# The last token group's first layer as pairs of 64-row matmuls into two banks

## The chip, the cores and the metric

One NeuronCore of a Trainium2 chip runs the whole program. The metric is the device time of one execution in microseconds. The kernel before has two recorded times, 681.75 and 683.06, with a median of 682.4.

## What is computed

Sparse attention over 4 batches, 8 heads, 768 positions and a head size of 64 feeds a two-layer block with 512 inputs, 2048 hidden units and 512 outputs. Cut to what matters here:

```python
x = attn_out.transpose(0, 2, 1, 3).reshape(3072, 512)   # tokens x model width
h = x @ w_in                                             # 512 -> 2048
sp = np.where(h > 20.0, h, np.log1p(np.exp(np.minimum(h, 20.0))))
g = h * np.tanh(sp)                                      # Mish
out = g @ w_out                                          # 2048 -> 512
```

The attention looks at a window of 16 positions to each side and at one summary (largest key, mean value) of each block of 32. It comes before the part that changes.

## The kernel before, in words

The 3072 tokens are twelve chunks of 256 (`CH`); two chunks make a token group of 512 (`TG`), so there are six groups, 0 to 5 (`NG`). The hidden width is cut into 16 blocks of 128 (`NFC`). A step is one group and one hidden block, 96 steps in all, group after group.

Precision comes from splitting. Each activation and each weight is held as a high and a low part of type float32r (`xh`, `xl`, `ah`, `al`, and weights `hi`, `lo`), and a product of two numbers is three matmuls: high by high, high weight by low activation, low weight by high activation.

For step (g, fc):

- `ff_in` (line 346) takes one PSUM tile `ph` of 128 x 512 from the pool `ps_w` and accumulates 12 matmuls into it on line 352: four pieces of 128 rows of the model width (`NCC`) by three products. The stationary operand is 128 x 128 of `w_in`, the moving operand 128 rows by 512 tokens of x. All 128 rows of the array are contracted at once.
- `ff_act` (line 356) applies Mish on ScalarE straight from `ph` into the tile `a` in SBUF, on line 359.
- `ff_split` (line 362) makes `ah` (a cast, line 368) and `al` (a subtraction on VectorE, line 370). From group 1 on both stand on VectorE.
- `ff_out` (line 372) does 12 matmuls on line 380, for four blocks of 128 tokens by three products. They accumulate over all 16 steps of the group into the four PSUM tiles `po` of the pool `ps_o`. After the last step of the group the results are copied out on line 388 and written by DMA on line 389.

The order of the work is written out by hand (`tc.manual_schedule()`): each engine works in the order of the code. The last loop (line 451) calls, for its index i, `ff_in` and `ff_act` of step i, then attention work for a later group where there is some, `ff_split` of step i, and `ff_out` of step i - 2. So on TensorE two steps' matmuls lie between a step's `ff_in` and its own `ff_out`: `ff_out(i-2)`, `ff_in(i+1)`, `ff_out(i-1)` and `ff_in(i+2)`, until the last steps, where `ff_in` has run out.

Attention for group g is worked off during group g - 1, so steps 80 to 95 (group 5) hold none of it. In the earlier groups three attention pieces stand between the long matmuls on TensorE: the scores (line 283: 64-row, 64-column pieces, where the two heads use the upper and the lower half of the array and write two PSUM tiles), the transposes (line 320) and the values (line 338: 120 rows, 64 columns). float32 matmuls of these lines run as two instructions each.

Each of the two PSUM pools has four tiles of one bank. The pool `ps_w` serves `ph` and the scores, transposes and values of the attention.

Of the kernel before, what the change touches and what calls it, by code (L numbers as in the profile page):

```python
# [9 lines left out]
F32 = mybir.dt.float32  # L10
# [3 lines left out]
AF = mybir.ActivationFunctionType  # L14
# [3 lines left out]
B, H, S, D = 4, 8, 768, 64  # L18
DM, DFF = 512, 2048
BLK, WIN = 32, 16  # L20
P = 128
# [9 lines left out]
NCC = DM // P  # L31
# [6 lines left out]
TG = CG * CH  # L38
NG = NCH // CG
# [17 lines left out]
def fused_kernel(ctx: ExitStack, tc: tile.TileContext, q0, qk, kt, v0, vw, vs, w_in, w_out, out):  # L57
    nc = tc.nc
# [10 lines left out]
    ps_w = ctx.enter_context(tc.tile_pool(name="ps_w", bufs=4, space=PS))  # L69
# [9 lines left out]
    for h in range(2):  # L79
        r = slice(h * QT, (h + 1) * QT)  # L80
# [23 lines left out]
    def weight(w, part, fc):  # L104

        group, k = (early, fc) if fc < EARLY else (late, fc - EARLY)
        return group[w][part][:, k, :]
# [60 lines left out]
    for part, step, at0 in ((blocks[:, :NQ], QT, -WIN), (blocks[:, NQ:], P, CH)):  # L168
        n = part.shape[1]
# [6 lines left out]
    part = blocks[:, :NQ]  # L176
# [166 lines left out]
    st = {}  # L343
    po = {}

    def ff_in(g, fc):
        xh, xl = xs[g]
        ph = ps_w.tile([P, TG], F32, tag="w", name=f"ph{g}_{fc}")
        wh, wl = (weight(0, part, fc) for part in range(2))
        for cc in range(NCC):  # L350
            for n, (w, x) in enumerate(((wh, xh), (wh, xl), (wl, xh))):
                nc.tensor.matmul(ph, w[:, cc * P:(cc + 1) * P], x[:, cc, :],  # L352
                                 start=(cc == 0 and n == 0), stop=(cc == NCC - 1 and n == 2))
        st[g, fc] = ph

    def ff_act(g, fc):

        a = ff.tile([P, TG], F32, tag="t", name=f"a{g}_{fc}", bufs=2)
        nc.scalar.activation(a, st[g, fc], AF.Mish)  # L359
        st[g, fc] = a  # L360

    def ff_split(g, fc):
# [33 lines left out]
    for u, unit in enumerate(todo[CG * HP:]):  # L396
        g, u = divmod(u, CG * HP)
# [15 lines left out]
    n = CG * HP  # L413
# [37 lines left out]
    for i in range(len(steps) + 2):  # L451
        upper_weight()
        if i < len(steps):
            ff_in(*steps[i])
            ff_act(*steps[i])
            if i < NFC:
                waiting.append(ff_split(*steps[i]))
# [72 lines left out]
```

## Time and profile before

| what | value |
|---|---|
| times recorded | 681.75 and 683.06 us, median 682.4 |
| span of the profiled execution | 680.6 us |
| TensorE matmul (PE) busy | 644.6 us, 95% |
| ScalarE (ACT) busy | 333.4 us, 49% |
| VectorE (DVE) busy | 291.1 us, 43% |
| mean granted TensorE clock over the span | 0.971 |
| stretch 585 to 668 us (most of group 5): granted clock | 1.00 |
| the same stretch: ACT busy, DVE busy | 10.18 us and 18.11 us of 83.00 |

The page names no time for the profiled execution other than its span, from the first to the last instruction; the recorded times lie 1.2 and 2.5 us above it.

A row of the timeline gives the start and the length of an instruction, or of a run of like ones with their count (x16), then engine, line, operation and tiles. PE is the matmul, PEld the load of its weights, which can run while an earlier matmul streams. A matmul's length reaches from its start until its last result is written; the next one may begin before that, so the distance from start to start tells what one costs in a row of them. In `128*128 128x512` the first pair is rows by columns of the weights, the second the moving operand. A bracket at the end gives the idle time before and what ended it.

### The profile page before, as it was taken

To read this page: it belongs to the slowest core of one execution; us is meant where nothing else is said; L and a number is where in the kernel's file an instruction comes from. 1 tells how busy PE (TensorE), PEld (TensorE's weight loads), DVE (VectorE), ACT (ScalarE), POOL (GpSimd) and SP (SyncE) were. 2 spreads that over 40 slices of the span, in tenths; PEclk is the share of its full clock that TensorE was granted. 3 is DMA by queue.
4 is the path that set the end of the run, shared out by engine and by line. 5 is a ranking of instruction groups with operands and counts; after the bars stand their busy time and mean duration, and the time that the engine had idled before them with its cause. 6 is when DMAs were issued, how large, how long until landed. Compare 5 with 4: busy or idle time off the path is not lost.

```text
span 680.6 us, 10882 instructions
## 1 busy us (share of the span) xinstructions
PE 644.6 (95%) x4160; PEld 514.8 (76%) x4160; DVE 291.1 (43%) x836; ACT 333.4 (49%) x722; POOL 67.5 (10%) x119
## 2 busy tenths in 40 slices
PE   4767888999999999999999999999999999999997
PEld 3546676777788788788788788788788788888886
DVE  3987889982332334442322344442232232221112
ACT  2766776685555545555545555545455445111111
POOL 3230001111010010010010010010010010000000
PEclk9967979899999999999999999999999999999999
DMA  8895556742141124351121144331141110010001
GB/s 290 235 301 180 192 177 233 240 122 87 51 146 46 50 71 153 116 175 46 50 85 45 48 134 152 117 114 45 45 152 45 45 60 1 15 47 0 1 1 62
DMA packets 31252, 71.05 MB, mean 104 GB/s; under 512 B 4832, under 2 KB 9952, under 8 KB 31200
## 3 DMA queue, kind: packets, MB, share of 16 engines
q1 hardware_dynamic: 31200, 70.35, 32.4%
q8 instruction: 33, 0.54, 0.4%
q14 instruction: 19, 0.16, 0.1%
HBM read 61.54 MB, written 6.29 MB: 100 GB/s over the span
## 4 chain that ended last, share of the span: by engine, by line
PE 82%; ACT 8%; DVE 4%; DMA 3%; issue 1%; SPq 0%; POOL 0%; POOLq 0%; ACTq 0%; DVEq 0%
PE po L380 37%; PE ph L352 35%; PE x_ps L338 4%; PE sc L283 3%; PE pt_ps L320 3%; ACT w_f L143 2%; DVE w_f L156 2%; DVE w_f L154 1%; DMA qk<-qk 1%; ACT pr L303 1%; DMA vw<-vm 1%; DMA vw<-vw 1%; ACT L359 1%; ACT L303 1%; ACT a L359 1%
## 5 line engine op out<-in xcount | busy, mean ns | idle before, releaser
L359 ACT ACTIVATE a<-ph 128x512 f32<-128x512 f32 x96 | 57.4, 598 | 155.9 <-PE ph L352 155.5
L368 DVE CAST ah<-a 128x512 fp32r<-128x512 f32 x80 | 34.0, 426 | 197.1 <-ACT a L359 197.1
L380 PE MATMUL po<-w_early_out_hi,ah 128*128 128x512 f32 x240 | 98.6, 411 | 0.0
L352 PE MATMUL ph<-xh,w_early_in_hi 128*128 128x512 f32 x240 | 97.8, 407 | 0.0
L359 ACT ACT_TABLE_LOAD x41 | 52.6, 1283 | 88.6 <-PE ph L352 88.4
L380 PE MATMUL po<-w_early_out_lo,ah 128*128 128x512 f32 x240 | 95.3, 397 | 0.0
L352 PE MATMUL ph<-xl,w_early_in_hi 128*128 128x512 f32 x240 | 95.0, 396 | 0.0
L352 PE MATMUL ph<-xh,w_early_in_lo 128*128 128x512 f32 x240 | 94.9, 395 | 0.0
L380 PE MATMUL po<-w_early_out_hi,al 128*128 128x512 f32 x240 | 94.7, 394 | 0.0
L314 POOL TENSOR_TENSOR pr<-pr,rs 128x480 f32<-128x480 f32 x48 | 48.2, 1005 | 421.7 <-DVE rs L313 361.1
L303 ACT ACTIVATE pr<-pr,nm 128x120 f32<-128x120 f32 x192 | 73.6, 384 | 9.7 <-DVE nm L298 9.1
L340 DVE TENSOR_TENSOR xl<-x_ps,xh 128x256 fp32r<-128x256 f32 x48 | 20.3, 423 | 118.1 <-ACT xh L339 118.0
L370 DVE TENSOR_TENSOR al<-a,ah 128x512 fp32r<-128x512 f32 x96 | 66.3, 691 | 2.7
L380 PE MATMUL po<-w_late_out_hi,ah 128*128 128x512 f32 x144 | 58.5, 407 | 0.0
L352 PE MATMUL ph<-xh,w_late_in_hi 128*128 128x512 f32 x144 | 57.6, 400 | 0.0
L380 PE MATMUL po<-w_late_out_lo,ah 128*128 128x512 f32 x144 | 57.0, 396 | 0.0
L380 PE MATMUL po<-w_late_out_hi,al 128*128 128x512 f32 x144 | 56.8, 394 | 0.0
L352 PE MATMUL ph<-xh,w_late_in_lo 128*128 128x512 f32 x144 | 56.2, 391 | 0.0
L352 PE MATMUL ph<-xl,w_late_in_hi 128*128 128x512 f32 x144 | 56.1, 390 | 0.0
L380 PEld LDWEIGHTS po<-w_early_out_hi,ah 128*128 128x128 f32 x240 | 45.9, 191 | 13.0 <-issue 4.1
L352 PEld LDWEIGHTS ph<-xh,w_early_in_lo 128*128 128x128 f32 x240 | 46.0, 192 | 10.2
L380 PEld LDWEIGHTS po<-w_early_out_lo,ah 128*128 128x128 f32 x240 | 45.8, 191 | 10.3
(74 smaller groups left out, 919.4 us busy)
## 6 DMA issues: line engine op xcount, KB each, us to landing
qk<-qk SPq DMA_DIRECT2D x44, 496.0 KB
vw<-vw SPq DMA_DIRECT2D x48, 192.0 KB
w<-w_in SPq DMA_DIRECT2D x16, 512.0 KB
w<-w_out SPq DMA_DIRECT2D x16, 512.0 KB
ks<-kt SPq DMA_DIRECT2D x17, 384.0 KB
out<-o SPq DMA_DIRECT2D x24, 256.0 KB
vsum<-vs SPq DMA_DIRECT2D x12, 384.0 KB
vw<-vm SPq DMA_DIRECT2D x48, 48.0 KB
```

The source lines that it names most:

```text
L143: nc.scalar.activation(f, high.bitcast(F32), AF.Copy, scale=2.0 ** -OFFSET)
L283: nc.tensor.matmul(ps[h][row, at0:at0 + KA], u["qk"][r, s, h * QT:(h + 1) * QT], u["qk"][r, s, P:], start=True, stop=True)
L303: nc.scalar.activation(pr[:, s, :], pr[:, s, :], AF.Exp, scale=-1.0, bias=nm[:, s:s + 1], accum_out=sm[:, s:s + 1])
L314: nc.gpsimd.tensor_mul(pr, pr, rs.unsqueeze(2).broadcast_to([P, NQ, KA]))
L320: nc.tensor.transpose(ps[:KA, s * P:(s + 1) * P], u["p"][:, s, :], ident)
L338: nc.tensor.matmul(x, u["v"][:, s, d], pt, start=True, stop=True)
L340: return lambda: nc.vector.tensor_sub(xl, ps[:, :CH], xh.bitcast(F32))
L352: nc.tensor.matmul(ph, w[:, cc * P:(cc + 1) * P], x[:, cc, :], start=(cc == 0 and n == 0), stop=(cc == NCC - 1 and n == 2))
L359: nc.scalar.activation(a, st[g, fc], AF.Mish)
L368: (nc.scalar.copy if g == 0 else nc.vector.tensor_copy)(ah, a)
L370: return lambda: nc.vector.tensor_sub(al, a, ah.bitcast(F32))
L380: nc.tensor.matmul(po[g][t], a[:, tok], w, start=(fc == 0 and n == 0), stop=(fc == NFC - 1 and n == 2))
```

## The change

Only group 5 (`g == NG - 1`) is touched. `ff_in` takes two PSUM tiles for a step. Each of the 12 matmuls with 128 rows becomes two with 64: rows 0 to 63 of weights and activations go into the first tile, rows 64 to 127 into the second. The two stand next to each other in the program. `ff_act` then copies the first tile to `a` on ScalarE, adds the second tile on VectorE, and applies Mish in place in SBUF. The sum over all 512 inputs is the same, ordered differently.

```diff
     def ff_in(g, fc):
         xh, xl = xs[g]
+        wh, wl = (weight(0, part, fc) for part in range(2))
+        if g == NG - 1:
+            ph = [ps_w.tile([P, TG], F32, tag="w", name=f"ph{g}_{fc}_{r}") for r in range(2)]
+            for cc in range(NCC):
+                for n, (w, x) in enumerate(((wh, xh), (wh, xl), (wl, xh))):
+                    for r in range(2):
+                        rows = slice(r * D, (r + 1) * D)
+                        nc.tensor.matmul(ph[r], w[rows, cc * P:(cc + 1) * P], x[rows, cc, :],
+                                         start=(cc == 0 and n == 0), stop=(cc == NCC - 1 and n == 2))
+            st[g, fc] = ph
+            return
         ph = ps_w.tile([P, TG], F32, tag="w", name=f"ph{g}_{fc}")
-        wh, wl = (weight(0, part, fc) for part in range(2))
...
     def ff_act(g, fc):
 
         a = ff.tile([P, TG], F32, tag="t", name=f"a{g}_{fc}", bufs=2)
-        nc.scalar.activation(a, st[g, fc], AF.Mish)
+        if g == NG - 1:
+            nc.scalar.copy(a, st[g, fc][0])
+            nc.vector.tensor_add(a, st[g, fc][1], a)
+            nc.scalar.activation(a, a, AF.Mish)
+        else:
+            nc.scalar.activation(a, st[g, fc], AF.Mish)
         st[g, fc] = a
```

TensorE, step 9 of group 5 before: the end of the `ff_out` of step 7 (that tile's name begins `po`), then `ff_in` into one tile.

```order
L380 MATMUL po_3_5509<-w_early_out_hi,al_6_5631 128x512
L380 MATMUL po_3_5509<-w_early_out_lo,ah_6_5630 128x512
L352 MATMUL ph_9_5708<-xh_4606,w_early_in_hi 128x512
L352 MATMUL ph_9_5708<-xl_4607,w_early_in_hi 128x512
L352 MATMUL ph_9_5708<-xh_4606,w_early_in_lo 128x512
L352 MATMUL ph_9_5708<-xh_4606,w_early_in_hi 128x512
```

TensorE in the change, at the same kind of place, step 3 of group 5. In a `ph` name the first number is the step, the second the half of the array.

```order
L395 MATMUL po_3_5554<-w_early_out_hi,al_0_5447 128x512
L395 MATMUL po_3_5554<-w_early_out_lo,ah_0_5446 128x512
L355 MATMUL ph_3_0_5567<-xh_4606,w_early_in_hi 128x512
L355 MATMUL ph_3_1_5568<-xh_4606,w_early_in_hi 128x512
L355 MATMUL ph_3_0_5567<-xl_4607,w_early_in_hi 128x512
L355 MATMUL ph_3_1_5568<-xl_4607,w_early_in_hi 128x512
L355 MATMUL ph_3_0_5567<-xh_4606,w_early_in_lo 128x512
L355 MATMUL ph_3_1_5568<-xh_4606,w_early_in_lo 128x512
```

Nothing changes its place; 24 matmuls stand where 12 stood, alternating between the halves, and the 12 of `ff_out` before and after them remain full-height.

VectorE before, at the last steps of group 5.

```order
L368 CAST ah_14_5878<-a_14_5876 128x512
L370 TENSOR_TENSOR al_14_5879<-a_14_5876,ah_14_5878 128x512
L368 CAST ah_15_5909<-a_15_5907 128x512
L370 TENSOR_TENSOR al_15_5910<-a_15_5907,ah_15_5909 128x512
L388 COPY o_5940<-po_1_5507 128x512
```

VectorE in the change, same steps.

```order
L371 TENSOR_TENSOR a_14_6099<-ph_14_1_6074,a_14_6099 128x512
L383 CAST ah_14_6103<-a_14_6099 128x512
L385 TENSOR_TENSOR al_14_6104<-a_14_6099,ah_14_6103 128x512
L371 TENSOR_TENSOR a_15_6145<-ph_15_1_6120,a_15_6145 128x512
L383 CAST ah_15_6149<-a_15_6145 128x512
L385 TENSOR_TENSOR al_15_6150<-a_15_6145,ah_15_6149 128x512
L403 COPY o_6180<-po_1_5552 128x512
```

One addition stands ahead of each step's cast; on ScalarE one copy stands ahead of each step's Mish in the same way.

## The prediction

> **What bounds the kernel now.** I read the page's busy times and its chain first, then the stage that the change touches.
>
> ```profile
> PE 644.6 (95%) x4160; PEld 514.8 (76%) x4160; DVE 291.1 (43%) x836; ACT 333.4 (49%) x722; POOL 67.5 (10%) x119
> ...
> PE 82%; ACT 8%; DVE 4%; DMA 3%; issue 1%; SPq 0%; POOL 0%; POOLq 0%; ACTq 0%; DVEq 0%
> ```
>
> The chain of work that ended last is 82% TensorE. In the stretch that changes it is TensorE throughout, as the view of stretches says.
>
> ```profile
> 585.00:668.00 83.00, 83.00 (x368) 68.73 (x367) 18.11 (x32) 10.18 (x17) 0.00 (x0) 1.00 0.04 13
> ```
>
> Its columns are length, PE, PEld, DVE, ACT, POOL, granted clock, DMA share, GB/s. PE is busy for all of the 83 us at clock 1.00, while DVE works 18 us and ACT 10. What is added on ACT and DVE has room; what is added on PE moves the end. The timeline of one step gives the price of a matmul.
>
> ```profile
> 654.80 0.39 PE L352 MATMUL ph<-xh,w_late_in_hi 128*128 128x512 f32 x1
> 654.81 0.19 PEld L352 LDWEIGHTS ph<-xl,w_late_in_hi 128*128 128x128 f32 x1
> 655.03 0.39 PE L352 MATMUL ph<-xl,w_late_in_hi 128*128 128x512 f32 x1
> ...
> 657.52 0.39 PE L380 MATMUL po<-w_late_out_hi,ah 128*128 128x512 f32 x1
> ```
>
> From the first of the 12 matmuls of `ff_in` to the first of `ff_out` it is 2.72 us, so one costs 2.72/12 = 0.2267 us. The next weights load while it streams (the load at 654.81, 0.19 us long, is done before 655.03) and cost nothing.
>
> **The change part by part. First, the pairs.** Out go 16 steps x 12 = 192 full-height matmuls, in come 192 pairs of half-height ones, and each half still streams 512 columns. If the halves of a pair run side by side, a pair costs about one matmul; if not, two. The trace has half-height pieces to judge by, the scores, beside the transposes, which use the whole array.
>
> ```profile
> 210.33 0.33 PE L283 MATMUL sc<-qk 64*64 64x120 f32 x3
> ...
> 210.33 0.64 PE L283 MATMUL sc<-qk 64*64 64x120 f32 x16
> ...
> L283 PE MATMUL sc<-qk x704: 262/263/459, 29.0 to 568.8; 64*64 64x120 f32 x176
> ...
> 577.33 0.60 PE L320 MATMUL pt_ps<-ident,pr 128*120 128x128 f32 x4
> ...
> L320 PE MATMUL pt_ps<-ident,pr 128*120 128x128 f32 x192 | 31.1, 287 | 4.0 <-POOL pr L314 4.0
> ```
>
> Four transposes of 128 columns take 0.60 us, and one alone 0.287, so they follow each other at (0.60 - 0.287)/3 = 0.104 us, or 0.81 ns a column. A score of 120 columns would then cost 0.098 us on one tile of the array, and 16 in a row 1.56 us. They start within 0.64 - 0.26 = 0.38 us, about 0.025 each. Four tiles therefore work at once, and two of those four differ only in the rows. The first row says it directly: in a window of 0.02 us three of them have begun. So halves do overlap in this kernel, loads included, since each of these matmuls has its own load.
>
> I take a pair at the price of one matmul, 0.2267 us: the pairs add 0. Bounds: a round of four scores is 4 x 0.025 = 0.100 us against 0.098; 0.002 to 0.003 more per pair adds 0.6 us at most. The values (16 in 0.69 us, one 0.22, two tiles at once, rows below) go at 0.47/15 x 2 = 0.063 per round of 64 columns against 64 x 0.81 = 0.052, 0.011 more; as a fixed sum per pair that adds 2.1 us, in proportion (20% of 0.2267) 8.7. Below nothing: if float32 passes each column in two beats, one beat for 512 columns would be 512 x 0.81/2 = 0.208 us, so the 0.2267 would hold 0.019 of overhead that a pair might shed, 192 x 0.019 = 3.6 us. This is an estimate from those rows. Range of the term: -3.6 to +8.7. I keep 0: the scores, the only pieces that share the array by rows, lie nearest to it.
>
> **Second, the changes of shape.** Each `ff_in` now goes from full height to half height and back. The nearest place in the trace is step 79, where the values alone stand between long matmuls.
>
> ```profile
> L338 PE MATMUL x_ps<-pt,vw x768: 222/222/369, 23.7 to 581.1; 120*64 120x64 f32 x192
> ...
> 580.30 0.39 PE L352 MATMUL ph<-xh,w_late_in_lo 128*128 128x512 f32 x1
> 580.62 0.69 PE L338 MATMUL x_ps<-pt,vw 120*64 120x64 f32 x16
> 581.23 0.50 PE L380 MATMUL po<-w_late_out_hi,ah 128*128 128x512 f32 x1
> 581.57 0.39 PE L380 MATMUL po<-w_late_out_hi,al 128*128 128x512 f32 x1
> ```
>
> From 580.30 to 581.57 it is 1.27 us. Taken off are two long matmuls (0.453) and the values themselves (8 rounds of 0.052 = 0.42): 0.40 us is left for going in and out. One sees where it sits: 580.62 comes 0.32 after a start that costs 0.227, and the first `po` takes 0.50 in place of 0.39, a load that is not hidden. 16 x 0.40 = 6.4 us, all on PE. Above: if the load of 128 columns at the way in costs more than the values' 64 (half of that 0.11 more), 0.45, or 7.2 us. Below: between transposes and `ff_in`, both full height, almost nothing is lost (from 577.33 to the second `ph` at 578.00: 0.67 - 4 x 0.104 - 0.227 = 0.03), so a shape change that counts as none costs 16 x 2 x 0.03 = 1.0 us.
>
> ```profile
> 578.00 0.39 PE L352 MATMUL ph<-xl,w_late_in_hi 128*128 128x512 f32 x1
> ```
>
> I take 6.4: the row with unequal shapes is the nearest.
>
> **Third, the longer way from `ph` to `al`.** Each step adds a copy on ACT and an addition on DVE, and Mish stands behind both.
>
> ```profile
> L388 ACT COPY o<-po 128x512 f32<-128x512 f32 x12 | 6.5, 578 | 6.8 <-PE po L380 6.7
> L388 DVE COPY o<-po 128x512 f32<-128x512 f32 x12 | 7.8, 678 | 5.6 <-PE po L380 5.6
> ...
> 668.18 0.39 PE L352 MATMUL ph<-xh,w_late_in_lo 128*128 128x512 f32 x1
> ...
> 668.94 0.60 ACT L359 ACTIVATE a<-ph 128x512 f32<-128x512 f32 x1 [5.13 <-PE ph L352]
> ...
> 670.03 0.69 DVE L370 TENSOR_TENSOR al<-a,ah 128x512 fp32r<-128x512 f32 x1
> ...
> 673.84 0.39 PE L380 MATMUL po<-w_late_out_hi,ah 128*128 128x512 f32 x1
> ```
>
> 0.58 + 0.69 + 0.1 for the hand-overs = 1.4 us more. The last step has the least room: `al` is ready at 670.72, its `ff_out` begins at 673.84, 3.1 us later. With 1.4 us more, 1.7 us are left, so the `ff_out` of the two steps before hides it. Elsewhere two `ff_in` lie in between as well. The two banks of a step must be empty two steps later, over 8 us after they fill; the addition has read the second one within 2. ACT's 16 x 0.58 = 9.2 us and DVE's 16 x 0.69 = 11.0 us fall into the idle time above. Nothing else is queued behind the new additions than the cast and the subtraction of their own step. If that cover were gone, each step would pay up to 1.4 us, 22 us in all. I take 0.
>
> **The sum.** The profiled span is 680.6; 680.6 + 0 + 6.4 + 0 = 687.0. The median of the runs shown lies 1.8 above that span, so the forecast is 682.4 + 6.4 = 688.8 us, 0.9% more. By the bounds: from 682.4 + 1.0 - 3.6 = 679.8 to 682.4 + 7.2 + 8.7 = 698.3. A measurement of this kernel tells about 2% from no change, that is 696.0.
>
> **Rivals. One: the halves of a pair don't overlap.** For it: results leave the array faster than anywhere in the trace. A full-height matmul gives 128 results per column at 0.443 ns a column (0.2267/512), 289 per ns; four score tiles give 4 x 64 per 0.81 ns, 316; a pair would give 256 per 0.443, 578. No row shows that rate, and none shows halves of type float32r. Against it: the scores' fourfold overlap. Its price: 192 x 0.2267 = 43.5 us, 732.3 with the shape changes. It decides as soon as a pair costs over 0.264 us, 0.037 more than one matmul, for then 6.4 + 192 x 0.037 is 13.6 us, the 2%.
>
> [...]
>
> **Two: the loads come out of hiding.** A pair needs two loads, and a half's next load may have to wait for that half's stream. The load that isn't hidden costs 0.50 - 0.39 = 0.11 us at 581.23. 192 x 0.11 = 21 us gives 709.9; if the two records of 0.19 follow each other and bind, 192 x (0.38 - 0.227) = 29 us gives 718. Against it: loads hide at 654.81, and 16 score loads keep up with 0.025 us a matmul. It needs that the two halves' loads share one path.
>
> [...]
>
> **Three: the shape changes cost next to nothing, and the pair sheds overhead.** 682.4 + 1.0 - 3.6 = 679.8 to 683. For it: 0.03 us after the transposes. Against it: 0.40 at step 79.
>
> **How the numbers follow.** The forecast (pairs overlap, shape changes paid) gets 0.75 with its own range of 684 to 694; rival one 0.13, rival two 0.06, rival three 0.06. Faster by over 2% would need under 668.8, which no case reaches: 0.01. Slower by over 2% are rivals one and two: 0.19. The rest, 0.80, is within 2%. The range 681 to 698 takes in the forecast, most of rival three and the upper bounds of the first two terms; outside are mainly the 0.19. Rival one's 0.13 covers a partial overlap too, a pair at anything from 0.264 to 0.453.
>
> **What would show it.** Right: in group 5 the two halves start within about 0.01 us of each other and pairs follow at 0.22 to 0.24; a gap of about 0.1 and a first matmul of about 0.50 at either edge of `ff_in`; a step of 5.44 + 0.40 = 5.84 us; no wait for `al` on PE. Wrong: halves 0.2 apart (rival one), loads of a pair one behind the other and pairs at 0.33 or more (rival two), no gaps (rival three), or PE idle before `po`, released by DVE.

## The result and the profile after

The changed kernel takes 691.7 us (two runs, 691.39 and 692.01) against 682.4; the ratio is 1.0136, with a 95% interval of 1.0107 to 1.0166. More runs of the same kernel, in the first experiment below, give 1.0104 (1.0084 to 1.0124). The forecast was 688.8, in a range of 681 to 698. The slowdown is clear of the run-to-run spread and stays under the 2% that the prediction named.

The page of the kernel after, engines and chain:

```profile
PE 651.7 (94%) x4352; PEld 511.6 (74%) x4352; DVE 301.8 (44%) x852; ACT 342.8 (50%) x738; POOL 69.3 (10%) x119
...
PE 82%; ACT 8%; DVE 4%; DMA 4%; issue 1%; SPq 0%; POOL 0%; POOLq 0%; ACTq 0%; DVEq 0%
```

192 matmuls more, and the chain is as much TensorE as before. The view of stretches over most of group 5 (columns as in the prediction):

```profile
586.00:684.00 98.00, 98.00 (x591) 72.34 (x591) 30.21 (x50) 20.49 (x34) 0.00 (x0) 1.00 0.03 11
```

PE is busy to the end at clock 1.00, and the page shows no gap: a matmul's record is 0.39 us long where the next one starts after 0.227, so short gaps between them don't appear as idle time. They have to be read from the starts. One step of group 5 on TensorE, from the timeline after:

```profile
656.65 0.39 PE L395 MATMUL po<-w_early_out_hi,al 128*128 128x512 f32 x1
656.88 0.39 PE L395 MATMUL po<-w_early_out_lo,ah 128*128 128x512 f32 x1
657.20 0.50 PE L355 MATMUL ph<-xh,w_late_in_hi 64*128 64x512 f32 x2
657.53 0.40 PE L355 MATMUL ph<-xl,w_late_in_hi 64*128 64x512 f32 x2
657.76 0.40 PE L355 MATMUL ph<-xh,w_late_in_lo 64*128 64x512 f32 x2
658.00 0.40 PE L355 MATMUL ph<-xh,w_late_in_hi 64*128 64x512 f32 x2
...
659.62 0.39 PE L355 MATMUL ph<-xl,w_late_in_hi 64*128 64x512 f32 x2
659.84 0.39 PE L355 MATMUL ph<-xh,w_late_in_lo 64*128 64x512 f32 x2
660.16 0.50 PE L395 MATMUL po<-w_late_out_hi,ah 128*128 128x512 f32 x1
660.50 0.40 PE L395 MATMUL po<-w_late_out_hi,al 128*128 128x512 f32 x1
...
663.13 0.50 PE L355 MATMUL ph<-xh,w_late_in_hi 64*128 64x512 f32 x2
```

Each row of line 355 is a pair (x2), no longer than a matmul alone (0.39 to 0.50 us, as the rows of line 395): the halves run side by side. A step, from 657.20 to 663.13, is 5.93 us; before it was 24 x 0.2267 = 5.44. The 0.49 us more has three parts at each of the two changes of shape. The distance from the last full-height start to the first pair is 0.32 in place of 0.227 (0.09 of gap). From the first pair to the second it is 0.33 (0.11 more than 0.227: the first loads aren't hidden). Then the pairs come a little late before they settle. From 657.53 to 659.84 there are ten intervals in 2.31 us, 0.231 each, 0.046 us more than ten at the old pace; I call this the slow rest. The same three parts follow at 660.16.

Where the whole difference lies can be read from two starts, those of the last values (step 79) and of the last matmul, in the kernel before and then in the one after:

```profile
580.62 0.69 PE L338 MATMUL x_ps<-pt,vw 120*64 120x64 f32 x16
...
676.34 0.39 PE L380 MATMUL po<-w_late_out_lo,ah 128*128 128x512 f32 x1
```

```profile
582.44 0.69 PE L338 MATMUL x_ps<-pt,vw 120*64 120x64 f32 x16
...
686.05 0.39 PE L395 MATMUL po<-w_late_out_lo,ah 128*128 128x512 f32 x1
```

This stretch took 95.72 us before and 103.61 after: 7.89 more, and 32 changes of shape make it 0.247 each. The other 1.82 us between the spans (690.3 and 680.6) lie ahead of 580.62, where the two programs do the same work. The starts here are rounded to 0.01 us.

### The profile page after: what moved, and what is told of

Its sections match the earlier page's. It is cut to its first block, busy times and chain, and to the rows that moved or that the text cites. A ratio compares the mean times of both kernels' runs of the same rounds, so it can differ in the third digit from the quotient of the medians.

```text
span 690.3 us, 11314 instructions
## 1 busy us (share of the span) xinstructions
PE 651.7 (94%) x4352; PEld 511.6 (74%) x4352; DVE 301.8 (44%) x852; ACT 342.8 (50%) x738; POOL 69.3 (10%) x119
## 4 chain that ended last, share of the span: by engine, by line
PE 82%; ACT 8%; DVE 4%; DMA 4%; issue 1%; SPq 0%; POOL 0%; POOLq 0%; ACTq 0%; DVEq 0%
PE po L395 37%; PE ph L362 28%; PE ph L355 7%; PE x_ps L338 4%; PE sc L283 3%; PE pt_ps L320 2%; ACT w_f L143 2%; DVE w_f L156 2%; DVE w_f L154 1%; DMA qk<-qk 1%; DMA vw<-vw 1%; ACT pr L303 1%; DMA vw<-vm 1%; ACT L374 1%; ACT L303 1%
## 5 line engine op out<-in xcount | busy, mean ns | idle before, releaser
L395 PE MATMUL po<-w_early_out_hi,ah 128*128 128x512 f32 x240 | 100.1, 417 | 0.0
L374 ACT ACTIVATE a<-ph 128x512 f32<-128x512 f32 x80 | 47.8, 597 | 79.9 <-PE ph L362 79.5
L362 PE MATMUL ph<-xh,w_early_in_hi 128*128 128x512 f32 x200 | 82.1, 410 | 0.0
L362 PE MATMUL ph<-xl,w_early_in_hi 128*128 128x512 f32 x200 | 79.7, 398 | 0.0
L362 PE MATMUL ph<-xh,w_early_in_lo 128*128 128x512 f32 x200 | 79.6, 398 | 0.0
L395 PEld LDWEIGHTS po<-w_early_out_hi,al 128*128 128x128 f32 x240 | 46.1, 192 | 8.7
L322 ACT COPY pt<-pt_ps 120x512 f32<-120x512 f32 x48 | 28.1, 585 | 44.0 <-PE pt_ps L320 43.7
L362 PE MATMUL ph<-xh,w_late_in_hi 128*128 128x512 f32 x120 | 48.3, 402 | 0.0
```

What stands on the lines that cost most here:

```text
L322: nc.scalar.copy(pt.rearrange("p s q -> p (s q)"), ps[:KA, :])
L395: nc.tensor.matmul(po[g][t], a[:, tok], w, start=(fc == 0 and n == 0), stop=(fc == NFC - 1 and n == 2))
```

## The experiments

The theory after the result: a change of shape costs 0.247 us, made of a gap, a first load that nothing hides, and a slow rest; pairs cost as much as single matmuls, and the sum of the two banks is hidden. The rivals: the copy and the addition slow TensorE; or a pair is a little dearer than a matmul; or the change also acts ahead of group 5. The column "stretch" is the distance from the start of the last values to the start of the last matmul, read as above from each kernel's profiled execution. Each ratio is against runs of the kernel before that were made beside it, so it isn't the quotient of the medians listed.

| kernel | median, us | ratio to before, interval | stretch, us | over 95.72 |
|---|---|---|---|---|
| before | 682.4 | | 95.72 | |
| changed, once more | 688.9 | 1.0104 (1.0084 to 1.0124) | 103.62 | 7.90 |
| full height, two banks | 682.3 | 1.0002 (0.9984 to 1.0021) | 95.73 | 0.01 |
| pairs, no sum | 689.45 | 1.0107 (1.0083 to 1.0131) | 103.62 | 7.90 |
| one half | 689.37 | 1.0118 (1.0092 to 1.0144) | 103.19 | 7.47 |
| small half-height matmul | 691.03 | 1.0128 (1.0100 to 1.0156) | 103.61 | 7.89 |
| small full-height matmul | 682.81 | 1.0029 (1.0010 to 1.0048) | 97.97 | 2.25 |
| all halves | 682.96 | 1.0021 (1.0005 to 1.0037) | 96.95 | 1.23 |
| two steps | 687.09 | 1.0069 (1.0045 to 1.0093) | 99.67 | 3.95 |
| twice the changes | 696.25 | 1.0202 (1.0171 to 1.0233) | 110.12 | 14.40 |
| rows outermost | 720.6 | 1.0563 (1.0526 to 1.0599) | 134.65 | 38.93 |
| blocks of three | 691.55 | 1.0137 (1.0094 to 1.0181) | 103.72 | 8.00 |
| blocks of six | 698.17 | 1.0243 (1.0204 to 1.0281) | 113.32 | 17.60 |

**The change once more.** No edit.

> The changed kernel once more, to part the change from what differs between runs by chance. Theory (each change of shape on TensorE costs 0.245 us: a gap of 0.09, a first load of 0.108 that nothing hides, and 0.046 for the slower matmuls after it; pairs and the sum of the banks cost nothing): 32 changes, 7.9 us in group 5, so 1.011 to 1.012 of before, the rest of the 9.3 us lying ahead of group 5 and by chance. Rival (the change also costs something ahead of group 5): 1.0136 again, 9.3 us.

The stretch repeats to 0.01 us, while the start of the last values moved to 578.88:

```profile
578.88 0.69 PE L338 MATMUL x_ps<-pt,vw 120*64 120x64 f32 x16
...
682.50 0.39 PE L395 MATMUL po<-w_late_out_lo,ah 128*128 128x512 f32 x1
```

Over the profiled executions here that start lies anywhere from 578.01 to 583.78, though every kernel does the same work up to it. The rival isn't borne out: it asked for 1.0136 again, which lies outside the new interval, and the kernels with the earliest and the latest start, 578.01 and 583.78, are two without any half-height pairs. Of the first comparison's 9.3 us, 7.9 are the change; the rest fits the scatter of the first 580 us.

**Full height, two banks.** The sum without halves.

```diff
-                    for r in range(2):
-                        rows = slice(r * D, (r + 1) * D)
-                        nc.tensor.matmul(ph[r], w[rows, cc * P:(cc + 1) * P], x[rows, cc, :],
-                                         start=(cc == 0 and n == 0), stop=(cc == NCC - 1 and n == 2))
+                    nc.tensor.matmul(ph[cc // 2], w[:, cc * P:(cc + 1) * P], x[:, cc, :],
+                                     start=(cc % 2 == 0 and n == 0), stop=(cc % 2 == 1 and n == 2))
```

> Group 5 with full-height matmuls, six into each of the two banks, and the copy and the addition as in the change: the sum of the banks without halves. Theory (shape changes are the cost): within 1 us of before. Rival (copy and addition slow TensorE, or come late): the 1.5 us of the change's group 5 that go beyond 32 x 0.2 appear here, 684 us, and matmuls of group 5 follow at 0.231 in place of 0.2267.

The view of stretches for this kernel:

```profile
585.00:668.00 83.00, 83.00 (x368) 68.71 (x367) 28.82 (x49) 19.35 (x32) 0.00 (x0) 1.00 0.04 13
```

DVE works 28.82 us in it where it worked 18.11 before, ACT 19.35 for 10.18, and PE keeps its pace: 0.01 us in the stretch. The sum is hidden and slows nothing.

**Pairs, no sum**, the other way about.

```diff
-            nc.scalar.copy(a, st[g, fc][0])
-            nc.vector.tensor_add(a, st[g, fc][1], a)
-            nc.scalar.activation(a, a, AF.Mish)
+            nc.scalar.activation(a, st[g, fc][0], AF.Mish)
```

> Pairs as in the change, but Mish reads the first bank alone; the second bank's half of the sum is left out, and so are the copy and the addition. Theory (shape changes): the same as the change within 0.5 us. Rival (the sum of the banks costs): 1.5 us less than the change.

The stretch is that of the change, 103.62. Both edits say the same, so the 1.5 us that group 5 costs beyond the forecast's 6.4 are not the sum's.

**One half**, from the kernel without the sum.

```diff
-                    for r in range(2):
+                    for r in range(1):
```

The second tile is not taken either.

> The change with the second matmul of each pair left out (rows 64 to 127 aren't contracted), and without the copy and the addition. Theory (the second half of a pair is free): the same as the change within 0.5 us. Rival (a pair costs more than one matmul): less by 192 x what the second half costs; at 0.005 us, 1 us less.

Without the second matmul of each pair the stretch shrinks by 0.43 us, which would be 0.002 us a pair. Most of it doesn't lie in the pairs, though. Behind each way back to full height, ten intervals take 2.31 us in the change, and 2.29 with one half (0.025 less before rounding). First the change, then one half:

```profile
660.50 0.40 PE L395 MATMUL po<-w_late_out_hi,al 128*128 128x512 f32 x1
...
662.81 0.39 PE L395 MATMUL po<-w_late_out_lo,ah 128*128 128x512 f32 x1
```

```profile
658.17 0.40 PE L393 MATMUL po<-w_late_out_hi,al 128*128 128x512 f32 x1
...
660.46 0.39 PE L393 MATMUL po<-w_late_out_lo,ah 128*128 128x512 f32 x1
```

16 x 0.025 = 0.40 of the 0.43 us sit there: the slow rest on the way back is shorter behind single matmuls. The second half itself costs next to nothing.

**A small half-height matmul in the kernel before**, and as its control **a small full-height one**.

```diff
         ph = ps_w.tile([P, TG], F32, tag="w", name=f"ph{g}_{fc}")
         wh, wl = (weight(0, part, fc) for part in range(2))
+        if g == NG - 1:
+            nc.tensor.matmul(ph[:, 0:128], wh[0:D, 0:P], xh[0:D, 0, 0:128], start=True, stop=True)
```

The control's line, under the same condition:

```diff
+            nc.tensor.matmul(ph[:, 0:128], wh[:, 0:P], xh[:, 0, 0:128], start=True, stop=True)
```

> The kernel before, with one small matmul of 64 rows and 128 columns ahead of each first layer of group 5, whose result is overwritten. Theory (shape changes): into half height 0.09 + 0.108, its own 0.057, back 0.245, so 16 x 0.50 = 8.0 us more than before, without any pair. Rival (pairs or the sum of the banks cost, a change of shape little): its own length alone, 16 x 0.057 = 0.9 us more.

> The control to the small matmul of 64 rows: the kernel before with a small matmul of 128 rows and 128 columns ahead of each first layer of group 5, whose result is overwritten. No change of shape. Theory (shape changes): its stream of 0.057 and the 0.05 by which the next load of 0.108 is longer than it, 16 x 0.11 = 1.8 us more than before. Rival (any short matmul breaks the flow as much): 8 us more, as with 64 rows.

The timeline around the small matmul (line 351), first the half-height one:

```profile
643.30 0.39 PE L382 MATMUL po<-w_early_out_lo,ah 128*128 128x512 f32 x1
643.62 0.32 PE L351 MATMUL ph<-xh,w_late_in_hi 64*128 64x128 f32 x1
643.87 0.50 PE L354 MATMUL ph<-xh,w_late_in_hi 128*128 128x512 f32 x1
644.21 0.39 PE L354 MATMUL ph<-xl,w_late_in_hi 128*128 128x512 f32 x1
```

```profile
642.64 0.39 PE L382 MATMUL po<-w_early_out_lo,ah 128*128 128x512 f32 x1
642.86 0.22 PE L351 MATMUL ph<-xh,w_late_in_hi 128*128 128x128 f32 x1
642.92 0.45 PE L354 MATMUL ph<-xh,w_late_in_hi 128*128 128x512 f32 x1
643.20 0.39 PE L354 MATMUL ph<-xl,w_late_in_hi 128*128 128x512 f32 x1
```

From the matmul ahead to the second long one behind it takes 0.91 us at half height and 0.56 at full height, where two long matmuls alone take 0.45. So 16 small matmuls of 64 rows do to the kernel before what the whole change does, 7.89 us. That the two agree to the hundredth is chance: the small matmul brings 0.057 us of its own (the distance of the two starts at 642.86 and 642.92, before rounding), the change has a second slow rest of 0.046 instead, and small differences make up the rest. The same ones with 128 rows cost 2.25, a little over the 1.8 expected. There is no gap ahead of them (642.64 to 642.86), but a slow rest behind: from 643.20 five intervals of 0.232, then the old pace.

**All halves.** Both layers as pairs; the bank of a block of tokens is `t % 2 * 2 + r`.

```diff
+        if g == NG - 1:
...
+                    for r in range(2):
+                        rows = slice(r * D, (r + 1) * D)
+                        nc.tensor.matmul(po[g][t % 2 * 2 + r], a[rows, tok], w[rows, :],
+                                         start=(fc == 0 and n == 0 and t < 2),
+                                         stop=(fc == NFC - 1 and n == 2 and t >= 2))
```

> Group 5 with both layers as pairs, so that the shape changes once and not 32 times. The second layer has four banks for two token blocks and adds the other two blocks into the same ones, so the outputs of group 5 are left unusable; 384 pairs in place of 384 matmuls. Theory (shape changes, pairs free): 0.3 us over before. Rival (pairs are slower than full-height matmuls by 0.005 us each): 2 us over before or more.

The stretch is 1.23 us over before, not 0.3, by a miscount of mine: in the first two steps of group 5 the second layer still works on group 4 at full height, so the shape changes five times, 5 x 0.247 = 1.23. Behind that the pairs go on at the pace of single matmuls:

```profile
629.65 0.39 PE L355 MATMUL ph<-xh,w_early_in_hi 64*128 64x512 f32 x2
...
631.69 0.39 PE L398 MATMUL po<-w_early_out_hi,ah 64*128 64x512 f32 x2
```

Nine pairs in 2.04 us are 0.2267 each.

**Two steps**, half the changes, and **twice the changes**, with the same matmuls in another order. First the core of the one, then that of the other.

```diff
+        if i >= len(steps) - NFC:
+            if i % 2 == 0:
+                for j in (i, i + 1):
+                    if j < len(steps):
+                        ff_in(*steps[j])
+                        ff_act(*steps[j])
+                        ff_split(*steps[j])()
+                for j in (i - 2, i - 1):
+                    ff_out(*steps[j])
+            continue
```

```diff
+        if len(steps) - NFC <= i < len(steps):
+            ff_in(*steps[i], range(0, 2))
+            ff_out(*steps[i - 2], range(0, 2))
+            ff_in(*steps[i], range(2, 4))
+            ff_act(*steps[i])
+            ff_split(*steps[i])()
+            ff_out(*steps[i - 2], range(2, 4))
+            continue
```

> The change with group 5's order in twos: two first layers, then two second layers, 16 changes of shape in place of 32, the same matmuls. Theory (shape changes): 16 x 0.245 = 3.9 us over before in group 5, 4 us under the change. Rival (a cost per step or per pair): as the change.

> The change with each first layer and each second layer of group 5 cut in two and interleaved, 64 changes of shape in place of 32, the same matmuls; six places between changes in place of twelve, so of the slow rest only the first six count (0.026 in place of 0.046). Theory (shape changes): 64 x (0.09 + 0.108 + 0.026) = 14.3 us over before. Rival (a cost per step or per pair): as the change, 8 to 9 us over before.

16, 32 and 64 changes cost 3.95, 7.89 and 14.40 us: 0.247, 0.247 and 0.225 each. The last is cheaper, as expected: only six places follow each change, and the slow rest is cut off. In the kernel with two steps one sees it end:

```profile
639.97 0.50 PE L355 MATMUL ph<-xh,w_late_in_hi 64*128 64x512 f32 x2
640.31 0.40 PE L355 MATMUL ph<-xl,w_late_in_hi 64*128 64x512 f32 x2
...
642.62 0.39 PE L355 MATMUL ph<-xh,w_late_in_lo 64*128 64x512 f32 x2
...
645.34 0.39 PE L355 MATMUL ph<-xh,w_late_in_lo 64*128 64x512 f32 x2
645.66 0.50 PE L395 MATMUL po<-w_early_out_hi,ah 128*128 128x512 f32 x1
```

From 640.31 to 642.62 ten intervals take 2.31 us, from 642.62 to 645.34 twelve take 2.72, which is 0.2267 again.

**Rows outermost**: does the overlap need the two halves side by side?

```diff
-            for cc in range(NCC):
-                for n, (w, x) in enumerate(((wh, xh), (wh, xl), (wl, xh))):
-                    for r in range(2):
+            for r in range(2):
+                for cc in range(NCC):
+                    for n, (w, x) in enumerate(((wh, xh), (wh, xl), (wl, xh))):
```

> The change with the loop over the halves outermost: twelve matmuls of the upper rows, then twelve of the lower, the same matmuls into the same banks. Theory (halves overlap only where they stand next to each other, since matmuls start in order): 16 x 12 x 0.2267 = 43.5 us on top of the change, 735 us. Rival (TensorE finds the other half's work further down its queue): as the change.

Neither came: the stretch is 31.04 us longer than the change's, 1.94 a step, or 8.6 places of 0.2267 in place of 12. The timeline shows how.

```profile
655.41 0.49 PE L355 MATMUL ph<-xh,w_early_in_hi 64*128 64x512 f32 x1
...
657.37 0.39 PE L355 MATMUL ph<-xh,w_early_in_lo 64*128 64x512 f32 x1
657.37 0.62 PE L355 MATMUL ph<-xh,w_early_in_hi 64*128 64x512 f32 x2
657.71 0.51 PE L355 MATMUL ph<-xl,w_early_in_hi 64*128 64x512 f32 x2
657.94 0.50 PE L355 MATMUL ph<-xh,w_early_in_lo 64*128 64x512 f32 x2
658.17 0.39 PE L355 MATMUL ph<-xh,w_early_in_hi 64*128 64x512 f32 x1
```

In the program the upper half's twelve run hi/xh, hi/xl, lo/xh four times over, then the lower half's do the same. The ninth of the upper half starts alone at 657.37. In the same hundredth the next row starts, two of hi/xh, followed by two of hi/xl: the lower half's first matmul (at 657.37) and second have started among the upper half's tenth and eleventh. So a matmul may start ahead of earlier ones in the program that wait for the other half, here ahead of three, and no more: until the ninth nothing of the lower half moved. The theory, that matmuls start in order, fell on that point, and two more kernels test a window of three.

**Blocks of three and blocks of six.**

```diff
             for cc in range(NCC):
-                for n, (w, x) in enumerate(((wh, xh), (wh, xl), (wl, xh))):
-                    for r in range(2):
+                for r in range(2):
+                    for n, (w, x) in enumerate(((wh, xh), (wh, xl), (wl, xh))):
```

```diff
-            for cc in range(NCC):
+            for cc, r in ((0, 0), (1, 0), (0, 1), (1, 1), (2, 0), (3, 0), (2, 1), (3, 1)):
                 for n, (w, x) in enumerate(((wh, xh), (wh, xl), (wl, xh))):
-                    for r in range(2):
+                    if True:
```

> The change with the halves in blocks of three: three matmuls of the upper rows, then three of the lower, four times a step. New theory (a matmul starts ahead of up to three earlier ones that still wait for the other half, so the halves overlap within a window of about four): as the change, 32 shape changes and no more than 1 us beside. Rival (matmuls start in program order): per block of six, four places in place of three, 16 x 4 x 0.2267 = 14.5 us on top of the change.

> The change with the halves in blocks of six, twice a step. New theory (window of about four): the lower half starts with the third or fourth of the upper, so it lags by two or three places, 16 x 2 to 3 x 0.2267 = 7 to 11 us on top of the change. Rival (program order): 21 places in place of 12, 16 x 9 x 0.2267 = 32.6 us on top.

Blocks of three cost 0.11 us more than the change in the stretch, blocks of six 9.71: 0.607 a step, 2.7 places. In the second the lower half starts with the upper half's fourth, ahead of three:

```profile
654.34 0.49 PE L355 MATMUL ph<-xh,w_late_in_hi 64*128 64x512 f32 x1
...
654.91 0.39 PE L355 MATMUL ph<-xh,w_late_in_lo 64*128 64x512 f32 x1
654.91 0.62 PE L355 MATMUL ph<-xh,w_late_in_hi 64*128 64x512 f32 x2
```

In blocks of three no matmul need go ahead of more than two. Program order, at 14.5 and 32.6 us, is out.

## Why the prediction was right, and where it was short

The likeliest case came true: pairs that overlap, and shape changes that are paid. Its size was off by 1.5 us in one term, and part of what came out right there was luck.

- **The pairs, 0 us.** Right. Leaving out the second half of every pair saves 0.43 us in all, pairs without shape changes follow at 0.2267, and rival one (43.5 us) is out. The score rows had it: four tiles that start within 0.02 us. The argument for the rival, that results would have to leave the array at 578 per ns, did not hold: pairs at 0.2267 us do deliver that. The 3.6 us that a pair might shed rested on an assumption of mine, two beats a column for float32, which no run shows; the pairs shed nothing.
- **Shape changes, 16 x 0.40 = 6.4 us.** This is the mis-sized term: 16 x 0.493 = 7.89, above its own upper bound of 7.2. The gap and the first load, 0.09 + 0.11 at each of 32 places, make the 6.4. What failed is that the row at step 79 was followed only to the second `po`, and the matmuls behind it were put at 0.2267, a pace taken from a place without breaks. The slow rest comes there, 0.046 us a change, 1.5 us in all. The trace of before had only part of it: five intervals of 0.232 from 581.57 on, and five behind the transposes from 578.00 on, 0.025 us each time.

```profile
581.80 0.40 PE L380 MATMUL po<-w_late_out_lo,ah 128*128 128x512 f32 x1
...
582.72 0.39 PE L380 MATMUL po<-w_late_out_hi,ah 128*128 128x512 f32 x1
```

By these rows the estimate would have been 16 x (0.40 + 2 x 0.025) = 7.2 us. That the 0.40 was right is in part luck. It took off eight rounds of values at 0.052 us, a rate derived from the transposes; the trace has the rounds 0.058 apart (the second starts at 580.72, the eighth at 581.07), which leaves 0.35. And the values' first load, of 64 columns, shows with 0.05 us, where the change's, of 128 columns, shows with 0.11. The one error made up for the other.

- **The sum of the banks, 0 us.** Right, shown from both sides. In the last step `al` is ready at 681.28, against an `ff_out` that starts at 683.56: 2.3 us to spare where 1.7 were forecast.

```profile
680.59 0.69 DVE L385 TENSOR_TENSOR al<-a,ah 128x512 fp32r<-128x512 f32 x1
...
683.56 0.39 PE L395 MATMUL po<-w_late_out_hi,ah 128*128 128x512 f32 x1
```

- **Rival two, loads out of hiding.** Out, but for the first of each run. The two loads of a pair run side by side: the next row has two in 0.18 us, and the median load of a half is 184 ns.

```profile
657.19 0.18 PEld L355 LDWEIGHTS ph<-xh,w_late_in_hi 64*128 64x128 f32 x2 [0.35 <-issue]
```

- **Rival three, cheap shape changes.** Out: the small full-height matmul costs 0.14 us, the half-height one 0.49. The transposes, with 0.03 us, were the wrong neighbour, for they keep the height of 128 rows (128*120 between 128*128).
- **The number.** 688.8 against 691.7 is the 1.5 us of the slow rest and 1.4 that fit the scatter ahead of group 5. The longer series (1.0104, 1.0084 to 1.0124) takes in the 1.0116 that 6.4 + 1.5 would give; that its median of 688.9 lies at the forecast is luck, for 7.9 us on top of the 682.3 measured beside it would be 690.2.

The gap is 0.09 us at 657.20, and ahead of the small full-height matmul at 642.86 there is none. It is less than half of the price of a change; the rest is the first load, 0.11, and the slow rest, 0.046.

## What to carry to other kernels

Half-height pairs are no faster than full-height matmuls (0.2267 us each here), so they gain nothing where 128 rows are there to contract; what they bring here is the price of changing shape, 0.25 us each time, so work of one shape should stand together. Price a break by following the rows until the old pace is back, not to the second instruction behind it. And read a difference from a stretch that starts behind whatever varies from run to run: the change's 103.61 repeats to 0.01 us, and the totals of the kernel before scatter from 679.1 to 684.4.

## What the runs showed of the hardware

- Half-height float32r pairs of 512 columns reach 0.2267 us a pair, the price of one full-height matmul of 128 rows, with both banks written at once (the two of a pair start within 0.01 us).
- A change between full height and pairs costs 0.247 us where at least twelve matmuls follow: 0.09 of gap, 0.11 of a load that isn't hidden, 0.046 of slower matmuls.
- Matmuls for one half of the array start up to three places ahead of earlier ones that wait for the other half: blocks of three overlap wholly (0.11 us), blocks of six lose 2.7 places a step, twelve and twelve 8.6. So matmuls here don't all start in program order: with rows outermost the lower half's first one starts at 657.37, ahead of the upper half's last three.
- After a break the long matmuls come at about 0.232 us, then at 0.2267, at a granted clock of 1.00 in the change (586 to 684 us) and before (577 to 584): nine intervals behind a change between full height and pairs (0.046 us in all), five behind the values, the transposes and a small full-height matmul (0.025), and four on the way back from single half-height matmuls (0.021). The transposes and the small full-height matmul change no height, so the slower pace doesn't need that. What makes it, and what sets its length, is open.
